# Pooling scores and pooling by 32-column operands into four row quarters of a bank, in an attention block fused with a rational feed-forward layer

## The chip, the cores and the metric

The kernel runs on one core of a Trainium2 chip. A core has five engines that work side by side, each with its own queue of instructions: TensorE (PE; its weight loads are listed apart as PEld), VectorE (DVE), ScalarE (ACT), GpSimd (POOL) and SyncE (SP), which issues all DMA transfers of this kernel in the order of its queue. The metric is the device time of one execution in microseconds (us), the median of several runs; lower is better.

## What is computed

Four batches (B=4) of N=12480 tokens with C=128 channels pass through an attention with m=32 inducing points, and then all 49920 tokens through a feed-forward layer of width 2048, whose activation is a quotient of two polynomials:

```python
def mab(q, kv):
    s = scale * (q @ kv.transpose(0, 2, 1))
    s = s - s.max(-1, keepdims=True)
    a = np.exp(s)
    a /= a.sum(-1, keepdims=True) + 1e-09
    return a @ kv
h = mab(I, x)            # pooling: 32 points attend to all tokens of a batch
x = mab(x, h)            # all tokens attend to the 32 pooled rows
...
h = x @ w_in
P = a[0] + a[1] * h + a[2] * h2 + a[3] * h3
Q = 1.0 + np.abs(b[0]) * np.abs(h) + np.abs(b[1]) * h2
g = P / (Q + 1e-06)
return (g @ w_out).astype(np.float32)
```

## The kernel before, in words

A batch is cut into 26 tiles of 480 tokens (BT; four chunks of TP=120), and tiles into groups of four (7 groups, the last with two tiles). The program has two stages.

**Boot** (`before`, lines 961 to 982, and the start of `main`): for batch 0 the pooling scores (`pass1`) and the pooling (`pooled`) are computed with nothing beside them, from wide tiles (xTw, xw); meanwhile the weights, 64-bit numbers in memory, are loaded (tiles `raw`) and converted on VectorE and POOL (`convert_weights`, with tiles cv). The loads are put between the steps of `pass1` and `pooled` by counts of those steps. `Params` loads moe_a and moe_b (tile `ab`) and VectorE derives the constants from them (tile `all`).

**Main** (`main`, `fast_ticks`): 832 units (4 batches, 26 tiles, 8 pairs of 128-wide slices of the 2048), one per tick. A unit's `first` makes hp with two f16 matmuls from the tile at (the attention weights of the tile's tokens, spread over 128 rows) and st (the pooled rows already multiplied by w_in); ACT, VectorE and POOL compute the activation (tiles u and l; ACT in turns Abs, Ln and Sigmoid); `second` adds two fp32 matmuls to po, the output bank. Once per tile VectorE copies po to oT and SP writes it to `out`.

Between the units of batch b stands side work, put there by `side` (line 780): two generators, `attend` (the tokens' attention: pd scores, pa transposes, hl, and eight copies of hl into at on SP's queue) and `ahead` (batch b+1: its pooling scores pc, the transposes pt, its pooling ph, then HT and the multiplication by w_in), announce before every step what it costs, as `yield "pe", 0.8`, in us of an engine, and `side` takes a step if the budget of that engine allows. PE's budget gains 0.75 per tick, keeps 2.5 at most, and 1.7 can be spent in a tick (line 193); so it is these costs that set the order. The side work's PSUM is one bank (`misc`), held by one generator at a time until `free`.

The two functions in question:

- `pass1` (line 370): the scores of four tiles come to stand below each other in one bank, pc, 32 rows each. Each tile's matmul writes all 128 rows, with a window of 128 columns out of `ind`, [128, 224], which is zero but for its 32 columns in the middle, and adds to what is there. VectorE takes the maximum (tile mxs) and copies to e.
- `pooled` (line 442): after the exponential (on ACT) four transposes (pt, copied to eT by ACT), then four matmuls per tile, one for each chunk, `eT` with 32 columns against the tile of 129 (128 channels and a column of ones that POOL's memset writes); all of a group add into ph[0:32], which VectorE adds to acc.

Tiles xTa (for pc) and x (for ph) are loaded in the order of use with four buffers, one tag: `columns` loads tile n+4 when tile n+1 is asked for, `x_rows` loads tile 4g+j+3 at tile 4g+j. So the load of a group's fourth tile is issued as the group's first matmul is. Before a group `landed` looks at the age of the fourth tile's load, in ticks, if it has been issued.

## Time and profile before

| | us |
|---|---|
| median of 3 runs | 2582.45 (2582.26 to 2583.76) |
| profiled execution | 2585.15 |
| its span, first to last instruction | 2583.0 |
| boot and the first units (to an Abs activation at 106.32) | 106.32 |
| units of batch 0, 1, 2 | 618.19, 624.43, 618.68 |
| units of batch 3 and the end | 615.38 |

| engine | busy us | share |
|---|---|---|
| PE | 2212.9 | 86% |
| DVE | 2219.0 | 86% |
| ACT | 2248.8 | 87% |
| POOL | 2070.8 | 80% |

The mean granted TensorE clock is 0.97 of full speed. The last stage has no work of a next batch in it; the three before it have. Nearly every instruction is recorded by one helper and shows as line 175, so tiles are the way to tell them apart. An engine's busy time does not tell what bounds the kernel; the windows below, cut at ACT's Abs activations (one for two units), tell what each engine does between them.

### The profile page before, as it was taken

The page shows a single profiled execution, that of the slowest core. Times are in us where ns is not written, and L with a number is a line of the kernel's source. Part 1 is how long each engine was busy: PE and PEld are TensorE (multiplying, and loading weights), DVE is VectorE, ACT ScalarE, POOL GpSimd, SP SyncE. Part 2 cuts the span into 40 slices and gives each one's busy share as a digit, 9 for nine tenths or more (in the row PEclk, how much of TensorE's full clock was granted, in tenths as well). Part 3 has the DMA queues.
Part 4 walks back from the last instruction along what each step waited for, and adds up shares of the span by engine and source line. Part 5 has one row for each costly group of instructions (what it writes and reads, how often), then busy time and mean ns, then how long its engine had stood idle before and what let it go on. Part 6 is the DMA issues. An engine that isn't in the chain of part 4 may idle for free.

```text
span 2583.0 us, 23703 instructions
## 1 busy us (share of the span) xinstructions
PE 2212.9 (86%) x7622; PEld 1074.2 (42%) x7622; DVE 2219.0 (86%) x2383; ACT 2248.8 (87%) x1591; POOL 2070.8 (80%) x1399
## 2 busy tenths in 40 slices
PE   8588987899889987998989989989878788788887
PEld 5344443454434443554534435544434334333333
DVE  2898998879889898889898989889989889888885
ACT  1388999988888899998898899998899999999995
POOL 0367789888868788888877887888788898899997
PEclk8689999999999999999998999999999999999999
DMA  9112210131112210221112202110101001000000
GB/s 249 54 58 80 71 37 16 38 77 43 31 45 75 76 39 13 56 62 43 42 58 69 65 23 54 51 49 27 49 13 46 20 15 31 15 17 18 12 15 17
DMA packets 117102, 120.88 MB, mean 47 GB/s; under 512 B 13289, under 2 KB 115561, under 8 KB 116969
## 3 DMA queue, kind: packets, MB, share of 16 engines
q1 hardware_dynamic: 116969, 119.28, 16.3%
q8 instruction: 62, 1.02, 0.2%
q14 instruction: 71, 0.58, 0.1%
HBM read 80.89 MB, written 25.56 MB: 41 GB/s over the span
## 4 chain that ended last, share of the span: by engine, by line
DVE 29%; PE 27%; POOL 21%; ACT 10%; issue 6%; DMA 1%; SPq 1%; DVEq 0%; POOLq 0%; ACTq 0%
DVE l L175 17%; PE po L175 16%; POOL l L175 15%; ACT u L175 8%; DVE u L175 6%; POOL u L175 5%; PE hp L175 4%; PE ph L175 2%; PE pd L175 2%; DVE oT L175 2%; ACT L175 2%; PE pc L175 1%; DVE asm L175 1%; SPq L175 1%; POOL a L175 1%
## 5 line engine op out<-in xcount | busy, mean ns | idle before, releaser
L175 PE MATMUL po<-l,w_out 128*128 128x480 f32 x3328 | 1485.6, 580 | 17.7 <-DVE oT L175 8.0
L175 POOL TENSOR_TENSOR l<-u 128x960 f32<-128x960 f32 x416 | 927.4, 2229 | 34.7
L175 PEld LDWEIGHTS po<-l,w_out 128*128 128x128 f32 x3328 | 627.3, 193 | 590.1 <-issue 457.2
L175 ACT ACTIVATE u<-u,all 128x1920 f32<-128x1920 f32 x416 | 775.5, 1888 | 1.2
L175 ACT ACTIVATE u<-u 128x1920 f32<-128x1920 f32 x416 | 737.5, 1797 | 8.2 <-POOL l L175 3.6
L175 POOL TENSOR_SCALAR l<-u,all 128x960 f32<-128x960 f32 x416 | 619.1, 1488 | 111.0 <-DVE u L175 105.1
L175 PE MATMUL hp<-at,st 128*128 128x480 f16 x1664 | 476.3, 374 | 266.7 <-DVE l L175 262.6
L175 DVE SCALAR_TENSOR_TENSOR l<-hp,all,l 128x960 f32<-128x960 f32 x416 | 504.1, 1212 | 185.3 <-POOL l L175 172.0
L175 POOL TENSOR_SCALAR u<-l,all 128x960 f32<-128x960 f32 x416 | 447.8, 1077 | 263.8 <-DVE l L175 229.3
L175 ACT ACTIVATE u<-hp,all 128x960 f32<-128x960 f32 x416 | 437.0, 1050 | 199.3 <-PE hp L175 180.6
L175 DVE SCALAR_TENSOR_TENSOR l<-l,all,u 128x960 f32<-128x960 f32 x416 | 575.0, 1383 | 1.7 <-ACT u L175 1.7
L175 DVE SCALAR_TENSOR_TENSOR l<-u,all,hp 128x960 f32<-128x960 f32 x416 | 500.1, 1202 | 6.2 <-ACT u L175 6.2
L175 DVE TENSOR_SCALAR u<-hp 128x960 int32<-128x960 int32 x416 | 475.7, 1144 | 17.6 <-PE hp L175 17.4
L175 PEld LDWEIGHTS <-st 128*128 128x128 f16 x1872 | 157.1, 100 | 711.4 <-DVE l L175 466.0
L175 ACT ACT_TABLE_LOAD x235 | 301.5, 1283 | 4.7 <-PEq L1056 0.7
L175 DVE COPY oT<-po 128x480 f32<-128x480 f32 x104 | 67.8, 652 | 81.5 <-PE po L175 81.3
L175 PEld LDWEIGHTS pd<-HT,xTb 128*120 128x120 f32 x832 | 102.5, 196 | 20.9 <-issue 9.1
L175 PE MATMUL pd<-HT,xTb 128*120 128x32 f32 x832 | 99.6, 275 | 7.0 <-DMA xTb<-x_c 6.1
L175 PE MATMUL ph<-x,eT 120*32 120x129 f32 x624 | 76.9, 274 | 3.5 <-DMA x<-x_t 3.5
L175 PE MATMUL pc<-xTa,ind 128*128 128x480 f32 x156 | 72.5, 570 | 5.6 <-DMA xTa<-x_c 2.8
L175 PEld LDWEIGHTS ph<-x,eT 120*32 120x32 f32 x624 | 64.9, 109 | 24.8 <-issue 16.3
L175 PE MATMUL po<-at,st 128*128 128x480 f16 x208 | 61.8, 380 | 0.0
(101 smaller groups left out, 685.9 us busy)
## 6 DMA issues: line engine op xcount, KB each, us to landing
xTb<-x_c SPq DMA_DIRECT2D x104, 240.0 KB, 2.9
out<-oT SPq DMA_DIRECT2D x104, 240.0 KB, 2.0
xTa<-x_c SPq DMA_DIRECT2D x78, 240.0 KB, 2.9
x<-x_t SPq DMA_DIRECT2D x78, 240.0 KB, 3.4
at<-hl SPq DMA_DIRECT2D x416, 30.0 KB, 1.8
xw<-x_t SPq DMA_DIRECT2D x8, 720.0 KB, 13.7
xTw<-x_c SPq DMA_DIRECT2D x5, 960.0 KB, 10.4
raw<-w_in SPq DMA_DIRECT2D x4, 480.0 KB, 11.7
```

Of the source, the lines that this page charges most:

```text
L175: ins = call(*args, **kw)
```

## The change

Three things. First, `ind` keeps only its 32 columns, and the four matmuls of a pc group write the four quarters of the bank's rows, each on its own (no accumulation, no zeros). They come after a single `yield "pe", 1.0` instead of four of 0.8, so that they stand in a row. Second, the four chunks of a tile in ph go to four quarters of the rows and accumulate over the tiles of the group; a tile announces 0.4 once where its four matmuls announced 0.2 each. acc has 128 rows, and at the end of a batch one matmul with `fold` (four identities of 32) adds the quarters: pq, from which the sum and H are read. Third, the counts by which boot puts the loads of weights between its steps are new, since there are fewer steps.

```diff
 
     def setup(self):
         nc, cp = self.nc, self.cp
-        self.ind = cp.tile([C, 7 * M], F32, name="ind")
-        nc.vector.memset(self.ind, 0.0)
-        nc.sync.dma_start(out=self.ind[:, 3 * M:4 * M], in_=self.ind_c)
+        self.ind = cp.tile([C, M], F32, name="ind")
+        nc.sync.dma_start(out=self.ind, in_=self.ind_c)
         self.ident = cp.tile([P, P], F32, name="ident")
         make_identity(self.tc.nc, self.ident)
         self.ones = cp.tile([1, 4], F32, name="ones")
...
         self.ident4 = cp.tile([M, 4, M], F32, name="ident4")
         for j in range(4):
             nc.vector.tensor_copy(out=self.ident4[:, j], in_=self.ident[0:M, 0:M])
+        self.fold = cp.tile([P, M], F32, name="fold")
+        for j in range(4):
+            rows = slice(M * j, M * j + M)
+            nc.vector.tensor_copy(out=self.fold[rows], in_=self.ident[rows, rows])
         self.many = cp.tile([M, 4], F32, name="many")
         nc.vector.memset(self.many, 1.0)
         self.w_max = cp.tile([C, 8], F32, name="w_max")
...
         for g in range(self.NG):
             nb = min(4, self.NB - 4 * g)
             yield from self.landed("a", b, g)
+            yield "pe", 1.0
+            pc = self.misc(f"pc{b}_{g}")
             for j in range(nb):
-                yield "pe", 0.8
-                if j == 0:
-                    pc = self.misc(f"pc{b}_{g}")
-                nc.tensor.matmul(pc[:, 0:BT], self.ind[:, M * (3 - j):M * (7 - j)], next(xs), start=(j == 0), stop=(j == nb - 1))
+                nc.tensor.matmul(pc[M * j:M * j + M, 0:BT], self.ind, next(xs), start=True, stop=True)
             rows = slice(0, M * nb)
             for i in range(2):
                 yield "v", 0.36
...
 
         nc, ap = self.nc, self.ap
         e = self.e[b]
-        acc = ap.tile([M, C + 1], F32, tag="acc", name=f"acc{b}")
+        acc = ap.tile([P, C + 1], F32, tag="acc", name=f"acc{b}")
         xs = self.xs.pop(b)
 
         def turned(g):
...
             yield from self.landed("x", b, g)
             for k in range(HB * nb):
                 j, c = divmod(k, HB)
-                yield "pe", 0.2
+                if c == 0:
+                    yield "pe", 0.4
                 if k == 0:
                     ph = self.misc(f"ph{b}_{g}")
                 if c == 0 and self.boot and (4 * g + j) % 3 == 0 and g + j:
...
                     self.wide_rows(b)
                 elif c == 0 and not self.boot and 0 < 4 * g + j < self.NB - 3:
                     xs.append(self.x_rows(b, 4 * g + j + 3))
-                nc.tensor.matmul(ph[0:M, 0:C + 1], eT[:, c, M * j:M * j + M], xs[4 * g + j][:, c, :], start=(k == 0), stop=(k == HB * nb - 1))
+                nc.tensor.matmul(ph[M * c:M * c + M, 0:C + 1], eT[:, c, M * j:M * j + M], xs[4 * g + j][:, c, :], start=(j == 0), stop=(j == nb - 1))
             yield "v", 0.2
             if g == 0:
-                nc.vector.tensor_copy(out=acc, in_=ph[0:M, 0:C + 1])
+                nc.vector.tensor_copy(out=acc, in_=ph[:, 0:C + 1])
             else:
-                nc.vector.tensor_tensor(out=acc, in0=ph[0:M, 0:C + 1], in1=acc, op=ALU.add)
+                nc.vector.tensor_tensor(out=acc, in0=ph[:, 0:C + 1], in1=acc, op=ALU.add)
             self.free()
-        yield "v", 0.2
+        yield "pe", 0.3
+        pq = self.misc(f"pq{b}")
+        nc.tensor.matmul(pq[0:M, 0:C + 1], self.fold, acc, start=True, stop=True)
+        yield "v", 0.4
         rs = ap.tile([M, 1], F32, tag="rs", name=f"rs{b}")
-        nc.vector.tensor_scalar(out=rs, in0=acc[:, C:], scalar1=1e-9, scalar2=None, op0=ALU.add)
+        nc.vector.tensor_scalar(out=rs, in0=pq[0:M, C:C + 1], scalar1=1e-9, scalar2=None, op0=ALU.add)
         nc.vector.reciprocal(out=rs, in_=rs)
         yield "v", 0.2
         H = ap.tile([M, C], F32, tag="H", name=f"H{b}")
-        nc.vector.tensor_scalar(out=H, in0=acc[:, 0:C], scalar1=rs, scalar2=None, op0=ALU.mult)
+        nc.vector.tensor_scalar(out=H, in0=pq[0:M, 0:C], scalar1=rs, scalar2=None, op0=ALU.mult)
+        self.free()
         yield "pe", 0.3
         pt = self.misc(f"HT{b}")
         nc.tensor.matmul(pt[:, 0:4 * M], H, self.ident4.rearrange("p a m -> p (a m)"), start=True, stop=True)
...
         self.setup()
         loads, words = self.weights(), []
         for n, _ in enumerate(self.pass1(0)):
-            if n >= 36 and n % 6 == 3:
+            if n >= 18 and n % 3 == 1:
                 words += [w for w in [next(loads, None)] if w]
         self.params = Params(self.tc.nc, self.cp, self.moe_a, self.moe_b)
         for n, _ in enumerate(self.pooled(0, self.cp.tile([C, 4 * M], F32, name="HT0"))):
-            if n % 20 == 5:
+            if n % 8 == 5:
                 words += [w for w in [next(loads, None)] if w]
         words += list(loads)
         self.params.derive()
```

What this does to the order. For batch 1 the scores' 7 groups begin 30 units into batch 0 and take 45 units before, 17 now; pooling's groups take 36 ticks before and 34 now; the multiplication by w_in starts 29, 47 and 68 units earlier for batches 1, 2 and 3. ACT's instructions are the same in number.

PE before, at the sixth group of batch 3's scores (pc3_5, tiles xTa3_20 to xTa3_23; hp2_4_7 is a unit of batch 2, tile 4):

```order
L175 MATMUL pc3_5_8260<-xTa3_20_8103,ind_74 128x480
L175 MATMUL pc3_5_8260<-xTa3_21_8118,ind_74 128x480
L175 LDWEIGHTS st_2_6700
L175 MATMUL hp2_4_7_8267<-at2_1_0_7888,st_2_6700 128x480
L175 LDWEIGHTS st_2_6700
L175 MATMUL hp2_4_7_8267<-at2_1_0_7888,st_2_6700 128x480
L175 MATMUL pc3_5_8260<-xTa3_22_8146,ind_74 128x480
L175 MATMUL pc3_5_8260<-xTa3_23_8261,ind_74 128x480
```

The group has a unit's hp between its second and third tile. PE after, at the same group, which now stands in batch 1's units, behind the last matmuls of po for tile 17:

```order
L175 MATMUL po1_17_0_6852<-at1_4_0_6144,st_1_3154 128x480
L175 LDWEIGHTS st_1_3154
L175 MATMUL po1_17_0_6852<-at1_4_0_6144,st_1_3154 128x480
L175 MATMUL pc3_5_6982<-xTa3_20_6934,ind_74 32x480
L175 MATMUL pc3_5_6982<-xTa3_21_6937,ind_74 32x480
L175 MATMUL pc3_5_6982<-xTa3_22_6940,ind_74 32x480
L175 MATMUL pc3_5_6982<-xTa3_23_6983,ind_74 32x480
L175 LDWEIGHTS st_1_3154
L175 MATMUL hp1_19_7_6993<-at1_4_1_6404,st_1_3154 128x480
```

All four now stand in a row, and the next unit's hp behind them. SP's queue at the loads of these tiles, before (out is a tile's result, at the eight copies of hl):

```order
L175 DMA xTa3_21_8118<-x_c 128x480
L175 DMA out<-oT2_1_8134 128x480
L175 DMA at2_1_1_8137<-hl2_1_7530 32x480 x8
L175 DMA xTa3_22_8146<-x_c 128x480
L175 DMA out<-oT2_2_8257 128x480
L175 DMA xTa3_23_8261<-x_c 128x480
L175 DMA xTa3_24_8264<-x_c 128x480
```

The copies stand ahead of the third tile's load, and one result between the third's and the fourth's. SP's queue at these loads, after:

```order
L175 DMA xTa3_20_6934<-x_c 128x480
L175 DMA xTa3_21_6937<-x_c 128x480
L175 DMA xTa3_22_6940<-x_c 128x480
L175 DMA out<-oT1_17_6970 128x480
L175 DMA at1_5_1_6973<-hl1_5_5949 32x480 x8
L175 DMA xTa3_23_6983<-x_c 128x480
L175 DMA xTa3_24_6986<-x_c 128x480
```

Now a result and the eight copies into at stand between the third tile's load and the fourth's, xTa3_23. At the sixth group of batch 3's pooling (ph3_5) it is the same, PE after:

```order
L175 MATMUL po2_3_0_8481<-at2_0_1_7718,st_2_6099 128x480
L175 LDWEIGHTS st_2_6099
L175 MATMUL po2_3_0_8481<-at2_0_1_7718,st_2_6099 128x480
L175 MATMUL ph3_5_8616<-x3_20_8516,eT3_5_8566 32x129 x4
L175 MATMUL ph3_5_8616<-x3_21_8523,eT3_5_8566 32x129 x4
L175 MATMUL ph3_5_8616<-x3_22_8530,eT3_5_8566 32x129 x4
L175 MATMUL ph3_5_8616<-x3_23_8617,eT3_5_8566 32x129 x4
```

All 16 matmuls stand in a row behind po's end; SP's queue after:

```order
L175 DMA x3_21_8523<-x_t 120x4x128
L175 DMA x3_22_8530<-x_t 120x4x128
L175 DMA out<-oT2_3_8604 128x480
L175 DMA at2_2_0_8607<-hl2_2_7756 32x480 x8
L175 DMA x3_23_8617<-x_t 120x4x128
```

where x3_23 stands behind out and the copies; before, these stood ahead of x3_21. At boot, SP's queue before (raw are weights, xw tiles of pooling, ab the activation's coefficients):

```order
L175 DMA raw0_177<-w_in 128x480
L175 DMA xw0_18_180<-x_t 120x12x128
L58 DMA ab_200<-moe_a 128x4
L59 DMA ab_200<-moe_b 128x2
L175 DMA raw1_216<-w_in 128x480
L175 DMA xw0_21_236<-x_t 120x12x128
L175 DMA raw2_244<-w_in 128x480
```

Between the first load of weights and the second stand ab and a tile of x; after:

```order
L175 DMA raw0_180<-w_in 128x480
L175 DMA xw0_18_184<-x_t 120x12x128
L175 DMA raw1_189<-w_in 128x480
L175 DMA raw2_199<-w_in 128x480
L58 DMA ab_208<-moe_a 128x4
L59 DMA ab_208<-moe_b 128x2
L175 DMA raw3_224<-w_in 128x480
L175 DMA xw0_21_244<-x_t 120x12x128
```

ab had one load of weights ahead of it and has three now.

## Rows read from the trace of the kernel before

**Rows 1.** The page: section 1 (each engine's busy time, share of the span, instructions) and the first line of section 4 (shares of the chain that ended last, by engine).

```profile
PE 2212.9 (86%) x7622; PEld 1074.2 (42%) x7622; DVE 2219.0 (86%) x2383; ACT 2248.8 (87%) x1591; POOL 2070.8 (80%) x1399
...
DVE 29%; PE 27%; POOL 21%; ACT 10%; issue 6%; DMA 1%; SPq 1%; DVEq 0%; POOLq 0%; ACTq 0%
```

**Rows 2.** Windows from one Abs activation of ACT to the fourth after it, nine of them near the end, with no work of the next batch in them. Columns: stretch, its length, busy time (and number) of PE, PEld, DVE, ACT, POOL, the granted clock, the DMA share, GB/s; the last line is sum and mean.

```profile
2415.95:2437.72 21.77, 17.65 (x50) 7.34 (x50) 19.02 (x18) 20.61 (x15) 20.26 (x13) 1.00 0.04 13
...
sum 195.77, PE 159.06 PEld 65.87 DVE 171.85 ACT 186.12 POOL 180.75; mean PE 17.67 PEld 7.32 DVE 19.09 ACT 20.68 POOL 20.08
```

**Rows 3.** The same view of the 18 such windows that hold matmuls of the pooling scores, the first from 173.38, the last to 1498.49; two of them and the sum.

```profile
872.98:899.38 26.40, 22.30 (x64) 10.18 (x63) 21.80 (x24) 21.16 (x17) 20.89 (x15) 0.94 0.20 61
...
1448.85:1475.05 26.20, 21.36 (x64) 9.54 (x65) 23.16 (x26) 21.17 (x16) 21.50 (x15) 1.00 0.21 65
...
sum 432.70, PE 392.13 PEld 184.16 DVE 394.56 ACT 384.38 POOL 348.78; mean PE 21.78 PEld 10.23 DVE 21.92 ACT 21.35 POOL 19.38
```

**Rows 4.** The same view of the 17 windows that hold matmuls of pooling, the first from 480.89; the last of them and the sum.

```profile
1684.59:1707.19 22.60, 22.29 (x96) 11.88 (x95) 18.77 (x19) 21.37 (x17) 20.29 (x16) 1.00 0.22 56
sum 392.63, PE 374.27 PEld 199.54 DVE 334.17 ACT 367.59 POOL 337.26; mean PE 22.02 PEld 11.74 DVE 19.66 ACT 21.62 POOL 19.84
```

**Rows 5.** Timeline of PE and its weight loads (PEld) at two pc matmuls. Columns: start, duration, engine, line, operation, out<-in, number of instructions run together.

```profile
895.49 1.77 PE L175 MATMUL pc<-xTa,ind 128*128 128x480 f32 x4
...
895.90 0.19 PEld L175 LDWEIGHTS pc<-xTa,ind 128*128 128x128 f32 x1 [0.21 <-issue]
896.30 0.19 PEld L175 LDWEIGHTS pc<-xTa,ind 128*128 128x128 f32 x1 [0.21 <-issue]
```

**Rows 6.** Timeline of the ph matmuls, at boot (32 instructions) and in the main stage (16, with a multiply by a wide operand before and after).

```profile
40.11 3.46 PEld L175 LDWEIGHTS ph<-xw,eT 120*32 120x32 f32 x32 [0.17 <-issue]
40.12 3.73 PE L175 MATMUL ph<-xw,eT 120*32 120x129 f32 x32
...
1688.45 1.96 PE L175 MATMUL ph<-x,eT 120*32 120x129 f32 x16
...
1690.34 0.58 PE L175 MATMUL hp<-at,st 128*128 128x480 f16 x2
```

**Rows 7.** The page, section 5, the ph matmuls of the main stage: operation, out<-in, count, busy time, mean ns of one, then idle time of PE before them and what ended it.

```profile
L175 PE MATMUL ph<-x,eT 120*32 120x129 f32 x624 | 76.9, 274 | 3.5 <-DMA x<-x_t 3.5
```

**Rows 8.** Timeline of VectorE: the maxima taken from the scores of four tiles (128 rows) and of two tiles (64 rows).

```profile
897.30 0.41 DVE L175 TENSOR_SCALAR_CACHE_REDUCE e<-pc 128x240 f32<-128x240 f32 x1 [0.58 <-PE pc L175]
...
909.53 0.39 DVE L175 TENSOR_SCALAR_CACHE_REDUCE e<-pc 64x240 f32<-64x240 f32 x1
```

**Rows 9.** Timeline at a pc group whose fourth tile came late: VectorE's copy of a result, SP's queue, PE, ACT. In brackets the idle time of the engine before it, and what ended it.

```profile
1464.16 0.65 DVE L175 COPY oT<-po 128x480 f32<-128x480 f32 x1
...
1464.84 0.35 SPq L175 DMA_DIRECT2D out<-oT  x1
...
1465.29 1.34 SPq L175 DMA_DIRECT2D xTa<-x_c  x3
...
1468.24 1.07 PE L175 MATMUL pc<-xTa,ind 128*128 128x480 f32 x2 [1.94 <-DMA xTa<-x_c]
...
1475.05 1.06 ACT L175 ACTIVATE u<-hp,all 128x960 f32<-128x960 f32 x1 [4.89 <-PE hp L175]
```

**Rows 10.** Timeline of SP's queue at the eight copies that spread `hl` into `at`.

```profile
1391.81 4.95 SPq L175 DMA_DIRECT2D at<-hl  x8
1396.86 0.53 SPq L175 DMA_DIRECT2D xTb<-x_c  x1
```

**Rows 11.** The page, section 6: DMA issues with their number, KB of one, and median us from issue to landing.

```profile
xTa<-x_c SPq DMA_DIRECT2D x78, 240.0 KB, 2.9
x<-x_t SPq DMA_DIRECT2D x78, 240.0 KB, 3.4
...
raw<-w_in SPq DMA_DIRECT2D x4, 480.0 KB, 11.7
```

**Rows 12.** Timeline of POOL's memsets of the ones column, with the ph matmuls between them.

```profile
1691.09 0.13 POOL L175 MEMSET x<- 120x4 f32 x2
...
1692.46 1.96 PE L175 MATMUL ph<-x,eT 120*32 120x129 f32 x16
...
1694.52 0.10 POOL L175 MEMSET x<- 120x4 f32 x1
```

**Rows 13.** Timeline of VectorE at boot: the first accumulation of pooling, the first instruction that reads `ab`, and the attention's first maximum.

```profile
39.64 0.28 DVE L175 COPY acc<-ph 32x129 f32<-32x129 f32 x1 [9.66 <-PE ph L175]
51.82 0.16 DVE L70 SCALAR_TENSOR_TENSOR all<-ab 128x1 f32<-128x1 f32 x1 [11.90 <-DMA ab<-moe_a]
...
93.72 0.69 DVE L175 TENSOR_REDUCE amx<-pd 120x16 f32<-120x512 f32 x1 [0.44 <-DVE w_out L175]
```

**Rows 14.** Windows at boot, columns as in rows 2.

```profile
28.00:32.00 4.00, 1.46 (x7) 1.22 (x8) 0.92 (x6) 1.99 (x3) 0.00 (x0) 0.86 1.13 183
...
64.00:68.00 4.00, 4.00 (x38) 3.96 (x38) 4.00 (x8) 0.38 (x1) 1.45 (x2) 1.00 1.09 351
```

**Rows 15.** Timeline of ACT and PE at an Abs activation that waited for hp.

```profile
898.71 0.97 PE L175 MATMUL hp<-at,st 128*128 128x480 f16 x4
...
899.38 1.06 ACT L175 ACTIVATE u<-hp,all 128x960 f32<-128x960 f32 x1 [2.57 <-PE hp L175]
```

## The prediction

> **What bounds the kernel now.** I read the page first: five engines are busy for 80 to 87% of the span, and the chain that ended last changes hands between VectorE (DVE), PE and GpSimd (POOL), ScalarE (ACT) being its fourth [rows 1]. So no engine's total decides; a stage must be read from who idles in it. Next I cut the span at the starts of ACT's Abs activations, which come once per two units, into windows of four such pairs, and sorted them by what side work lies in them. In nine windows near the end, with none of batch b+1's work, a window is 21.75 us and ACT is busy for 20.68 of it [rows 2]: ACT is the bound, with 1.07 us idle, and PE has 21.75 − 17.67 = 4.08 us to spare, 0.51 us in each of eight ticks. In the 18 windows with pooling scores (pc), ACT idles 432.70 − 384.38 = 48.3 us, where 18 calm windows would have 19.3: an **excess of 29.0 us** [rows 3]. In the 17 with pooling (ph) it idles 25.0 us against 18.2: an excess of 6.8 us [rows 4]. These 36 us are what faster side work can win at most. Not all of the 29 is PE's: in the pc windows VectorE is busy for 91%, with pooling's maxima and with the attention's own quotients, which the change leaves alone.
>
> **Scores (pc).** A pc matmul is two load-and-multiply pairs of 0.40 us each (a multiply from 895.49, the loads inside it at 895.90 and 896.30) [rows 5], so 0.80 us, and four tiles take 3.2 us whether they stand together or not. After, each writes one quarter of the bank's rows. No row shows two matmuls side by side in the array, so the bounds are: all four at once, 0.80 us; none, 3.2 us. I take the middle, because a matmul's two pairs use one quarter and must follow each other, while the second pair of one and the first of the next may overlap: five steps of 0.40, 2.0 us. Going from a wide operand to a 32-column one and back costs about 0.09 us each way: 16 pooling instructions take 1.96 us of PE in the main stage, where 32 took 3.73 without a change of width, 1.87 per 16 [rows 6]; so 2.19 us per group. The 6.5 groups of a batch then need 14.2 us. The built order puts them into 17 units of batch 1 where they took 45, and 17 ticks have 17 × 0.51 = 8.7 us of room. What is not covered is 5.5 us per batch, 16.5 in three; against 29.0 that is **−12.5 us** (all four at once: 6.4 us of work, all covered, and I keep 4 us for VectorE's share: −25; none: 22.2 us of work, 13.5 uncovered per batch: +11.5). VectorE's two maxima per group also come closer together; they are charged to its own budget as before, and the 4 us that I keep in the best case are for them. That HT is ready earlier in the order wins nothing here: I price it at 0.
>
> As for the array, the Trainium skill ("TensorE: Matmul & The Clock Gate", Part 3: Packing small matmuls — row/col tiling) lets tiles in different column quarters run side by side and gives a measured 2.38 times for three; no run here shows it yet, and by it a group would take 3.2 / 2.38 = 1.3 us, an estimate, and the sum would lie between the forecast and rival B. The same part, "What overlaps and what doesn't", speaks against this change: weight loads are said to lie beside a running multiply only if its rows differ, and all four operands here use the same rows. The trace disagrees: loads that use the same 128 rows as the multiply in progress start inside it [rows 5], so I give that rule no price of its own; if it held, the result would be rival D's.
>
> **Pooling (ph).** 16 matmuls are 32 instructions in 3.73 us [rows 6], 3.5 to 3.9 with the switch. In quarters the same overlap gives 17 × 0.11 + 0.19 = 2.06 us, a gain of 1.8 us of PE for each of some 20 groups. The excess is 6.8 us [rows 4], and PE's 3.5 us of waiting for x tiles [rows 7] are in it, so I take **−5 us** (0 to −7). VectorE's `acc` now adds 128 rows instead of 32; its time goes by the columns, as the maxima show: 0.41 us for 128 rows, 0.39 for 64 [rows 8], so 0. The new matmul `pq`, one per batch, has 129 columns as two of ph's instructions have, 0.23 us, and hands over through the bank that HT takes next; for three batches I count 0, at most 1 us.
>
> **Fourth tiles.** What it costs is that four matmuls now stand in a row, while the load of the fourth tile is issued as late as before, when the group begins. In the built order this falls behind the writing of a result and eight copies of `hl` at two places: `xTa3_23` and `x3_23`. Before, a late tile of this kind stopped PE for 1.94 us and ACT for 4.89 us at 1468–1475 [rows 9], so a stop of PE is not forgiven. The chain there: from the end of po, VectorE's copy until the queue issues, 0.68 us; the issue of `out`, 0.45 us with its gap [rows 9]; the eight copies, 4.95 and a gap of 0.1 [rows 10]; the landing, 2.9 us for xTa and 3.4 for x [rows 11]: 9.1 and 9.6 us. Three tiles' own matmuls cover 4 × 0.40 + 0.09 = 1.7 us of it, and 13 × 0.11 + 0.09 = 1.5. So PE stops for 7.4 and 8.1 us: **+15 us**. At five more places (`pc1_1`, `pc2_5`, `ph1_2`, `ph1_3`, `ph2_4`) the issue is one `out` and a landing away, 0.68 + 0.45 + 2.9 less 1.7, 2.3 us, or up to two ticks are between; I estimate 1 to 3.6 us each, 12 in all, and leave them to the range (+15 to +27; and down to +4, if hp is so far ahead that ACT has work). At `ph2_4` POOL's memset for `x2_19` also moves behind a unit's operations in its queue; memsets come 2.1 to 2.6 us after the ph before them starts [rows 6, 12], so it waits for POOL as much as for the load, and the 3.6 us covers both.
>
> **Boot.** The loads of weights come earlier by the new counts, and `ab` falls behind two more of 480 KB [rows 11]. VectorE has waited 11.90 us for `ab` at 51.82 and works from then on to 93.72, when the attention's maximum begins [rows 13], the conversions of the weights in between: what delays `ab` delays the end of boot. Two such loads are 983,040 bytes, at 183 to 351 GB/s [rows 14] 2.8 to 5.4 us; the engines of the DMA are full there (share 1.13 and 1.09), so an earlier issue does not bring the bytes sooner. Four accumulations, 0.28 us each as the first [rows 13], that stood behind `ab` now stand ahead of it, −1; acc5, acc6 and pq wait for PE between conversions, +1. **+4 us** (+2 to +6). The faster scores and pooling of boot bring nothing, as VectorE's work is behind `ab`. The constants (no memset of `ind`, four copies for `fold`) are early in VectorE's queue, ahead of a wait of 9.66 us [rows 13]: 0.
>
> **The sum.** 2582.45 + 4 − 12.5 − 5 + 15 = 2584 us. The profiled execution took 2585.15 us, 2.7 above the median, so differences are taken from it and put on the median. What can be told from no change is 0.2%, 5.2 us: this is 0.06%.
>
> **Rivals.**
> A, the forecast: pairs overlap, two fourth tiles stop PE. 2573 to 2595 by the bounds of boot (±2), of ph (+5, −2) and of the fourth tiles (−11, +4 of the smaller places). Chance 0.40, within it faster 0.08, same 0.26, slower 0.06.
> B, four quarters at once and fourth tiles mostly covered: pc −25, ph −7, tiles +4, boot +4: 2559 us. For it: the group is then 1 us, below two ticks' room. Against: the eight copies are in the queue whatever PE does. Chance 0.28, faster.
> C, **the late loads decide**: all seven fourth tiles stop PE in full, +27, pooling wins nothing since its tile is what it waits for: 2582.45 + 4 − 12.5 + 27 = 2601. It decides wherever the chain of the fourth load (4 us, or 9 with copies) is longer than the three matmuls ahead of it (1.5 to 1.8 us); below that it is nothing. For it: 1.94 us of waiting took 4.89 us from ACT [rows 9]. Against: ACT waited for hp for 2.57 us elsewhere with no tile late [rows 15], so a part of the 4.89 was due to other work. Chance 0.20, slower.
> D, the change does not do what it says: quarters of one bank run one after the other. A group is 3.4 us in one tick, charged as 1.0 by the planner. pc +11.5, ph 0, tiles 15 less 7 as each burst covers 1 us more, boot +4: 2606. For it: no row shows two matmuls at once. Chance 0.12, slower.
>
> **How the numbers follow.** The likeliest is A, so 2584 us. Faster 0.28 + 0.08 = 0.36; same 0.26; slower 0.06 + 0.20 + 0.12 = 0.38. The range goes from 2557, which leaves out about a third of B, to 2604, which leaves out D and little of C: 2 in 10 in all. A's own range is 2573 to 2595.
>
> **What will show it.** Pairs: the four pc multiplies of a group span 2.0 us; B: under 1.1; D: 3.2. In the pc windows ACT's excess falls to some 16 us. At the groups `pc3_5` and `ph3_5` PE idles 7 to 8 us until a DMA, at others 1 to 3. The wait of VectorE for `ab` ends near 55 us and the attention's maximum begins near 98. The forecast is wrong if the fourth tiles stop PE for under 4 us in all, or if boot ends no later than before, or if the pc group takes 3 us.

## The result and the profile after

| kernel | median us | ratio to before, 95% interval |
|---|---|---|
| before | 2582.36 (2579.63 to 2583.76, 4 runs) | |
| changed | 2606.69 (2603.27 to 2613.05, 4 runs) | 1.0098 (1.0075 to 1.0122) |

The change makes the kernel slower by 1.0%, 24 us. The profiled execution of the changed kernel took 2603.95 us, its span 2602.0; against the span before of 2583.0 that is 19.0 us to explain. The page after, busy time of the engines and the chain that ended last, answers to [rows 1]:

```profile
PE 2131.8 (82%) x7630; PEld 984.1 (38%) x7630; DVE 2228.4 (86%) x2386; ACT 2247.4 (86%) x1591; POOL 2053.1 (79%) x1399
...
DVE 33%; POOL 22%; PE 20%; ACT 13%; issue 7%; DMA 2%; SPq 2%; DVEq 0%; POOLq 0%; ACTq 0%
```

PE has 81 us less to do (2212.9 before), ACT as much as before and VectorE 9 us more, and yet the time is longer: PE idles 100 us more (370 before, 470 after). Where, the same cut by stage tells: boot, and the units of batches 0, 1 and 2 (batch 3 is unchanged at 615.4). Columns as in rows 2. Before:

```profile
0.00:106.32 106.32, 70.73 (x341) 48.61 (x341) 50.91 (x224) 13.91 (x24) 17.24 (x30) 0.79 0.73 179
106.32:724.51 618.19, 542.95 (x1977) 272.96 (x1977) 546.64 (x560) 555.23 (x396) 486.03 (x340) 0.97 0.17 50
724.51:1348.94 624.43, 551.56 (x1923) 269.71 (x1924) 553.52 (x576) 564.10 (x399) 513.74 (x354) 0.98 0.17 49
1348.94:1967.62 618.68, 549.11 (x1904) 267.69 (x1903) 547.69 (x552) 561.50 (x397) 508.24 (x350) 0.97 0.16 45
```

After:

```profile
0.00:113.40 113.40, 45.84 (x343) 24.09 (x343) 52.00 (x227) 13.90 (x23) 16.57 (x30) 0.62 0.69 168
113.40:750.97 637.57, 546.58 (x2037) 259.94 (x2038) 566.97 (x606) 556.21 (x397) 476.50 (x344) 0.94 0.20 58
750.97:1376.53 625.56, 530.09 (x1921) 246.51 (x1920) 549.82 (x561) 568.38 (x402) 501.61 (x354) 0.96 0.17 48
1376.53:1986.56 610.03, 510.71 (x1852) 238.17 (x1850) 538.55 (x522) 554.85 (x392) 512.97 (x345) 0.97 0.12 35
```

Boot is 7.1 us longer, batch 0 19.4, batch 1 1.1, and batch 2 8.7 us shorter. The column behind POOL's is the granted clock, and it fell: 0.97, 0.98, 0.97 before, 0.94, 0.96, 0.97 after, and at boot 0.79 before, 0.62 after. With 0.5 as the lower level (1.2 GHz of 2.4), a mean of 0.94 over 637.57 us is 12% of it, some 76 us, at half speed; 0.97 over 618.19 is some 37.

**The quarters do run at once.** Timeline of PE, a pc group of four tiles (eight instructions, with their weight loads) and a ph group (32):

```profile
194.30 0.16 PEld L175 LDWEIGHTS pc<-xTa,ind 128*32 128x32 f32 x8 [0.40 <-PE po L175]
194.30 1.01 PE L175 MATMUL pc<-xTa,ind 128*32 128x480 f32 x8
...
420.90 1.09 PE L175 MATMUL ph<-x,eT 120*32 120x129 f32 x32
```

1.01 us and 1.09 us, where before four tiles took 3.2 us (worked out in the prediction from [rows 5]) and 32 instructions 3.73 [rows 6]. That is rival B's price, not the forecast's 2.0 and 2.06.

**The waits.** The two groups of PE's instructions, with its idle time ahead of them in the last column and what ended it; first pc before, then pc and ph after:

```profile
L175 PE MATMUL pc<-xTa,ind 128*128 128x480 f32 x156 | 72.5, 570 | 5.6 <-DMA xTa<-x_c 2.8 <-DVE hl L175 1.8 <-issue 1.0
L175 PE MATMUL pc<-xTa,ind 128*32 128x480 f32 x156 | 31.5, 584 | 12.8 <-DMA xTa<-x_c 12.8
L175 PE MATMUL ph<-x,eT 120*32 120x129 f32 x624 | 25.3, 284 | 40.8 <-POOL x L175 26.8 <-DMA x<-x_t 13.6 <-ACT eT L175 0.4
```

Before, ph had 3.5 us [rows 7], with pc's 5.6 some 9 in all. After, it is 53.6 us, half of it for POOL, and nearly all of it is in the middle of bursts: in each of the 15 groups of pooling from a batch's second to its sixth PE stops ahead of the fourth tile, for 0.18 to 9.82 us, 13 times until POOL and twice until a DMA. One such stop, a group of pooling in batch 0 (SPq is SP's queue):

```profile
436.34 0.87 PE L175 MATMUL ph<-x,eT 120*32 120x129 f32 x24
436.88 2.39 SPq L175 DMA_DIRECT2D x<-x_t  x3
437.28 2.23 POOL L175 TENSOR_TENSOR l<-u 128x960 f32<-128x960 f32 x1
...
439.45 0.20 POOL L175 MEMSET x<- 120x4 f32 x4
...
439.60 0.66 PE L175 MATMUL ph<-x,eT 120*32 120x129 f32 x8 [2.40 <-POOL x L175]
...
440.19 3.10 PE L175 MATMUL po<-l,w_out 128*128 128x480 f32 x4
...
443.80 1.06 ACT L175 ACTIVATE u<-hp,all 128x960 f32<-128x960 f32 x1 [2.85 <-PE hp L175]
```

Three tiles' 24 instructions run at 436.34; the load of the fourth is issued at 436.88, and its memset stands in POOL's queue behind a 2.23 us operation of a unit. PE waits 2.40 us, released by POOL. And then the four instructions of po from 440.19 take 3.10 us instead of the 1.77 that four of po took at 434.63: PE had idled, and the clock that it is granted is down (0.66 on average from 440 to 444, below). ACT waits 2.85 us for hp behind it. Of the 15 stops eight were followed by such slow instructions, and the length of the stop alone does not tell which: behind another of 2.40 us, at 925.07, the four of po took 1.88. The other kind, the sixth group of batch 3's scores, of which the built order showed the loads:

```profile
1218.56 1.01 PE L175 MATMUL pc<-xTa,ind 128*32 128x480 f32 x6
...
1219.67 0.34 SPq L175 DMA_DIRECT2D out<-oT  x1
...
1220.07 4.95 SPq L175 DMA_DIRECT2D at<-hl  x8
...
1225.05 1.53 SPq L175 DMA_DIRECT2D xTa<-x_c  x3
...
1227.94 1.81 PE L175 MATMUL pc<-xTa,ind 128*32 128x480 f32 x2 [8.38 <-DMA xTa<-x_c]
...
1230.76 1.06 ACT L175 ACTIVATE u<-hp,all 128x960 f32<-128x960 f32 x1 [8.97 <-PE hp L175]
```

A result, eight copies in 4.95 us, and only then the load: PE stops for 8.38 us and ACT for 8.97. Windows of 4 us behind the first stop and over the second (the clock is the third column from the end):

```profile
440.00:444.00 4.00, 4.00 (x17) 1.81 (x10) 2.54 (x3) 1.15 (x2) 2.69 (x3) 0.66 0.27 69
1220.00:1224.00 4.00, 0.00 (x0) 0.00 (x0) 1.83 (x2) 1.80 (x1) 2.55 (x2) 1.00 0.32 100
1224.00:1228.00 4.00, 0.06 (x1) 0.06 (x2) 0.00 (x0) 0.00 (x0) 0.00 (x0) 0.54 0.51 148
1228.00:1232.00 4.00, 4.00 (x7) 1.31 (x8) 2.21 (x4) 1.24 (x2) 0.19 (x1) 0.60 0.36 121
```

At the second stop the clock falls to 0.54 while PE idles, and it is still 0.60 on average in the 4 us in which PE is wanted without a gap. In the windows with pc (ten now) and in those with ph (seventeen) the sums, answering to [rows 3] and [rows 4], are

```profile
sum 240.62, PE 216.60 PEld 90.65 DVE 216.14 ACT 210.77 POOL 180.86; mean PE 21.66 PEld 9.06 DVE 21.61 ACT 21.08 POOL 18.09
...
sum 411.79, PE 346.62 PEld 162.41 DVE 346.82 ACT 370.64 POOL 325.30; mean PE 20.39 PEld 9.55 DVE 20.40 ACT 21.80 POOL 19.14
```

pc: ACT idles 29.9 us, 10.7 of it natural, an excess of 19 instead of 29. ph: 41.2 us against 18.2, an excess of 23 instead of 6.8. What the scores won (10 us), pooling lost (16); boot comes on top. That is 13 of the 19.0 us; the other 6 are not traced to a place. VectorE at boot, the first use of `ab` and the attention's first maximum, against [rows 13]:

```profile
55.03 0.29 DVE L175 TENSOR_TENSOR acc<-ph,acc 128x129 f32<-128x129 f32 x1 [6.91 <-PE ph L175]
58.40 0.16 DVE L70 SCALAR_TENSOR_TENSOR all<-ab 128x1 f32<-128x1 f32 x1 [3.08 <-DMA ab<-moe_a]
...
100.74 0.69 DVE L175 TENSOR_REDUCE amx<-pd 120x16 f32<-120x512 f32 x1 [0.44 <-DVE w_out L175]
```

`ab` comes 6.6 us later than before, and the first maximum 7.0 us.

### The profile page after: what moved, and what is told of

Same layout as the page of the kernel before. It is cut to its first block, busy times and chain, and to the rows that moved or that the text cites. A ratio compares the mean times of both kernels' runs of the same rounds, so it can differ in the third digit from the quotient of the medians.

```text
span 2602.0 us, 23736 instructions
## 1 busy us (share of the span) xinstructions
PE 2131.8 (82%) x7630; PEld 984.1 (38%) x7630; DVE 2228.4 (86%) x2386; ACT 2247.4 (86%) x1591; POOL 2053.1 (79%) x1399
## 4 chain that ended last, share of the span: by engine, by line
DVE 33%; POOL 22%; PE 20%; ACT 13%; issue 7%; DMA 2%; SPq 2%; DVEq 0%; POOLq 0%; ACTq 0%
DVE l L175 19%; POOL l L175 16%; PE po L175 12%; ACT u L175 11%; DVE u L175 7%; POOL u L175 5%; PE hp L175 3%; ACT L175 2%; SPq L175 2%; DVE oT L175 2%; PE pd L175 2%; DVE asm L175 1%; DMA xTw<-x_c 1%; DVE cv L175 1%; DVE st L175 1%
## 5 line engine op out<-in xcount | busy, mean ns | idle before, releaser
L175 PEld LDWEIGHTS po<-l,w_out 128*128 128x128 f32 x3328 | 634.6, 195 | 603.2 <-issue 464.6
L175 POOL TENSOR_SCALAR l<-u,all 128x960 f32<-128x960 f32 x416 | 607.2, 1460 | 108.8 <-DVE u L175 107.5
L175 DVE SCALAR_TENSOR_TENSOR l<-l,all,u 128x960 f32<-128x960 f32 x416 | 585.2, 1407 | 1.7 <-ACT u L175 1.7
L175 PEld LDWEIGHTS pd<-HT,xTb 128*120 128x120 f32 x832 | 103.5, 198 | 20.1 <-issue 10.6
L175 PE MATMUL ph<-x,eT 120*32 120x129 f32 x624 | 25.3, 284 | 40.8 <-POOL x L175 26.8
L175 ACT ACTIVATE a<-a 120x512 f32<-120x512 f32 (+2 forms) x21 | 14.9, 728 | 41.2 <-DVE a L175 41.0
L175 POOL TENSOR_TENSOR cv<-cv 128x384 f32<-128x384 f32 (+2 forms) x11 | 12.1, 1096 | 48.5 <-DVE cv L175 47.0
```

Of the source, the lines that this page charges most:

```text
L175: ins = call(*args, **kw)
```

## The experiments

Theory: late fourth tiles (by the transfer and by POOL's memset) stop PE inside its bursts, and the clock that is granted after a stop adds to it; boot adds 7 us. Rivals: a PE with less to do gets less clock by itself; or side work pushed together costs, at VectorE. Each kernel is compared with the kernel before on the same chip, so ratios are compared. A tenth of a per cent is 2.6 us; by the intervals, a difference between two of these ratios is uncertain by 0.2 to 0.3%, 5 to 7 us.

| run | median us | ratio to before, 95% interval |
|---|---|---|
| e2_fourth_early | 2559.38 | 0.9903 (0.9887 to 0.9919) |
| e3_memset_late | 2576.87 | 0.9984 (0.9972 to 0.9997) |
| e9_fill | 2594.38 | 1.0061 (1.0045 to 1.0078) |
| e10_before_early | 2571.73 | 0.9968 (0.9958 to 0.9977) |
| e13_scores_early | 2566.41 | 0.9934 (0.9919 to 0.9948) |
| e4_scores_alone | 2587.53 | 1.0016 (1.0002 to 1.0030) |
| e5_pooling_alone | 2588.27 | 1.0010 (0.9997 to 1.0022) |
| e1_ab_back | 2606.02 | 1.0078 (1.0059 to 1.0097) |
| e7_both | 2551.43 | 0.9898 (0.9881 to 0.9915) |
| e8_before_ab_first | 2579.60 | 0.9980 (0.9968 to 0.9992) |
| e11_weights_early | 2566.37 | 0.9927 (0.9912 to 0.9942) |
| e12_weights_last | 2552.09 | 0.9876 (0.9857 to 0.9895) |

**e2_fourth_early.** In `columns`, `pass1` and `pooled`:

```diff
                 if n + 4 < self.NB:
                     ts.append(self.x_columns(b, n + 4, kind))
+                if kind == "a" and n % 4 == 3:
+                    yield None
...
                 nc.tensor.matmul(pc[M * j:M * j + M, 0:BT], self.ind, next(xs), start=True, stop=True)
+            if nb == 4 and not self.boot:
+                next(xs)
...
-                elif c == 0 and not self.boot and 0 < 4 * g + j < self.NB - 3:
+                elif c == 0 and not self.boot and j and 4 * g + j < self.NB - 3:
                     xs.append(self.x_rows(b, 4 * g + j + 3))
...
+            if not self.boot and 4 * g + 7 < self.NB:
+                xs.append(self.x_rows(b, 4 * g + 7))
             yield "v", 0.2
```

> The changed kernel, but the load of a group's fourth tile (and for pooling POOL's memset of its ones) is issued right behind the last matmul of the group before, not with the first matmul of its own. Theory (late fourth tiles cost the time): PE's idle time inside the bursts of the main stage, 12.8 us in pc and 38 in ph, falls below 5 us, and the time by 25 to 40 us, to 2567 to 2582; the granted clock's low stretches in the main stage, 162 us in the trace of the changed kernel against 108 before, go back with them to 100 to 120 us. Rival 1 (a PE that is less busy is granted less, whether it waits in bursts or not): the waits go but the low stretches stay near 160 us, and the time falls by 15 to 20 only, 2587 to 2592. Rival 2 (side work pushed together is what costs, VectorE above all): within 5 us of 2606.

Measured: 2559.38, 1.0% faster than before and 2% faster than the changed kernel; more than expected. Its groups of PE's instructions:

```profile
L175 PE MATMUL pc<-xTa,ind 128*32 128x480 f32 x156 | 22.1, 581 | 0.0
L175 PE MATMUL ph<-x,eT 120*32 120x129 f32 x624 | 21.9, 277 | 2.2 <-ACT eT L175 1.3 <-DMA x<-x_t 0.9
```

The waits are gone. By stage:

```profile
0.00:112.69 112.69, 47.28 (x343) 24.41 (x343) 51.77 (x227) 14.02 (x24) 17.20 (x30) 0.62 0.69 170
112.69:730.14 617.45, 526.06 (x1987) 253.71 (x1987) 558.29 (x576) 555.15 (x397) 481.14 (x341) 0.95 0.18 51
730.14:1336.16 606.02, 525.72 (x1966) 238.56 (x1966) 552.37 (x590) 562.05 (x396) 505.20 (x356) 0.99 0.21 59
1336.16:1941.32 605.16, 511.56 (x1854) 236.56 (x1854) 547.79 (x522) 560.07 (x395) 514.30 (x346) 0.98 0.13 36
```

Boot is as in the changed kernel; batches 0, 1 and 2 are 20.1, 19.5 and 4.9 us shorter than there, 44.5 in all, for 51.4 us fewer of waiting (53.6 less 2.2). The clock is back to 0.99 and 0.98 in batches 1 and 2; in batch 0 it stays at 0.95, which late tiles don't explain. Over the main stage the stretches at the lower level (low stretches, from here on) fall from 162 us in the changed kernel to 118, as the theory said; before they were 108. Rival 2 falls: the side work is pushed together as much. Rival 1 falls for batches 1 and 2, where PE has as little to do as in the changed kernel (525.7 and 511.6 us). The windows with pc (16) and ph (16):

```profile
sum 371.59, PE 323.53 PEld 137.06 DVE 348.42 ACT 342.07 POOL 300.49; mean PE 20.22 PEld 8.57 DVE 21.78 ACT 21.38 POOL 18.78
...
sum 353.95, PE 313.64 PEld 144.08 DVE 322.92 ACT 345.66 POOL 311.24; mean PE 19.60 PEld 9.00 DVE 20.18 ACT 21.60 POOL 19.45
```

pc: 29.5 us idle, 17.1 natural, an excess of 12; ph: 8.3 us, less than the 17.1 of as many calm windows.

**e3_memset_late.** As e2, but the memset of the fourth x tile stays with the first matmul of its group:

```diff
-        self.nc.gpsimd.memset(t[:, :, C:], 1.0)
+        if ones:
+            self.nc.gpsimd.memset(t[:, :, C:], 1.0)
...
+                elif c == 0 and not self.boot and j == 0 and 0 < 4 * g < self.NB - 3:
+                    nc.gpsimd.memset(xs[4 * g + 3][:, :, C:], 1.0)
...
-                xs.append(self.x_rows(b, 4 * g + 7))
+                xs.append(self.x_rows(b, 4 * g + 7, False))
```

> As e2_fourth_early, but POOL's memset of the fourth x tile's ones stays where the changed kernel has it, with the first matmul of its group; only the transfer is early. Theory (the memset is a part of the cost of its own, behind POOL's two operations of some 2 us each): PE idles for 20 to 35 us inside the ph bursts of the main stage, released by POOL, and the time is 8 to 20 us above e2_fourth_early, 2567 to 2580. Rival (the transfers are the whole cost; the memset's waits are covered by ACT's work in hand): within 4 us of e2_fourth_early's 2559.

Measured: 0.8% above e2 in the ratio, 21 us, and

```profile
L175 PE MATMUL ph<-x,eT 120*32 120x129 f32 x624 | 25.2, 285 | 29.9 <-POOL x L175 27.7 <-ACT eT L175 2.2
```

with 27.7 us of waiting for POOL. So the late memsets cost some 21 us where no transfer is late, and late transfers on top of them the rest up to the changed kernel, 1.0098 − 0.9984 = 1.1%, 29 us. The transfers late without the memsets were not run.

**e9_fill.** Work that adds zero (matmuls by `zero`, a tile of zeros) in the place of the waits, ahead of the fourth tile's matmuls:

```diff
+                if c == 0 and j == 3 and g and not self.boot:
+                    for i in range(32):
+                        rows = slice(M * (i % 4), M * (i % 4) + M)
+                        nc.tensor.matmul(ph[rows, 0:C + 1], self.zero, xs[4 * g + 2][:, i % 4, :], start=False, stop=False)
                 nc.tensor.matmul(ph[M * c:M * c + M, 0:C + 1], eT[:, c, M * j:M * j + M], xs[4 * g + j][:, c, :], start=(j == 0), stop=(j == nb - 1))
```

> The changed kernel with 32 matmuls by a tile of zeros ahead of the fourth tile's in every ph group but a batch's first and last: some 1.8 us of work for PE, which adds zero, in a place where it waits 1.4 to 9.8 us in 16 of 18 groups. Nothing waits for less. Theory (part of the cost is the clock that is granted less after PE has idled): low stretches in the main stage before batch 3 fall from 150 us to under 125, and the time by 4 to 15 us, to 2592 to 2602. Rival (the wait itself is all the cost): the time is 2604 to 2612, the fill adding a little where it outlasts the wait, with or without a change of the low stretches.

Measured: 0.4% faster than the changed kernel, 9 to 10 us, with 29 us of useless work added to PE:

```profile
L175 PE MATMUL ph<-x,zero 120*32 120x129 f32 x960 | 29.1, 273 | 0.0
L175 PE MATMUL ph<-x,eT 120*32 120x129 f32 x624 | 24.8, 280 | 20.6 <-DMA x<-x_t 14.0 <-POOL x L175 5.3 <-ACT eT L175 1.1
```

The same group as in the fence of the memset above:

```profile
432.81 0.87 PE L175 MATMUL ph<-x,eT 120*32 120x129 f32 x24
...
433.49 1.94 PE L175 MATMUL ph<-x,zero 120*32 120x129 f32 x64
...
435.94 0.22 POOL L175 MEMSET x<- 120x4 f32 x4
...
436.12 0.43 PE L175 MATMUL ph<-x,eT 120*32 120x129 f32 x8 [0.69 <-POOL x L175]
...
436.48 1.88 PE L175 MATMUL po<-l,w_out 128*128 128x480 f32 x4
```

The fourth tile's matmuls start 3.31 us after the group's first ones, 3.26 in the changed kernel: the wait is as long. Over all 15 groups that have the fill (not 18, as the expectation has it) these times add to 58.1 us, 4.7 more than in the changed kernel. But the four instructions of po behind this one take 1.88 us and not 3.10, and slow ones follow one of the 15 groups only, the one in which a stop of 8.29 us is left behind the fill. The low stretches of batches 0 to 2 fall from 150 us to 126 (under 125 was expected), and batch 0, where they fall most (75 to 55), is the one that becomes clearly shorter (637.6 to 628.7 us). So a part of the cost is the clock, at least about a fifth (9.5 of 50 us, with some 7 us of uncertainty): the fill leaves the scores' stops as they were (12.3 us) and takes time itself.

**e10_before_early and e13_scores_early.** The same early loads in the kernel before, and in the kernel before with the scores' part of the change (e4, below). In e10:

```diff
                 nc.tensor.matmul(pc[:, 0:BT], self.ind[:, M * (3 - j):M * (7 - j)], next(xs), start=(j == 0), stop=(j == nb - 1))
+            if nb == 4 and not self.boot:
+                next(xs)
...
-                elif c == 0 and not self.boot and 0 < 4 * g + j < self.NB - 3:
+                elif c == 0 and not self.boot and j and 4 * g + j < self.NB - 3:
...
+            if not self.boot and 4 * g + 7 < self.NB:
+                xs.append(self.x_rows(b, 4 * g + 7))
```

> The kernel before, with wide windows and its own order of steps, and only the loads of the fourth tiles issued early as in e2_fourth_early. Theory (quarters give a gain of their own, early loads the rest): PE's waits for x tiles, 9 us in pc and ph of before, go, and the time falls by 4 to 12 us, to 2570 to 2579. Rival (the gain of e2_fourth_early over before is all from early loads): 2555 to 2564.

> e4_scores_alone with the early loads of the fourth tiles of e2_fourth_early: the scores in quarters, pooling as before, nothing late. Theory (the scores' quarters carry most of the gain, as ACT's excess was 29 us in the windows of pc and 6.8 in those of ph): ratio to before 0.990 to 0.993, near e2_fourth_early's 0.9903 although pooling is as it was, boot being 6 us shorter here. Rival (both parts carry it alike): 0.994 to 0.997, near e10_before_early's 0.9968.

Measured: 0.9968 and 0.9934. The first is as the theory expected: late fourth tiles cost the kernel before 8 us too. Against e4 (1.0016), which has the same scores with late tiles, e13 is 0.8%, 21 us, faster for some 11 us of PE's waiting that is gone (11.5 in pc, 0.8 now in ph), and the low stretches of the main stage fall from 136 to 100 us: here the waits cost more than their length. The second is between what the two expected: the scores' quarters are worth 0.3%, 9 us, and the way from there to e2, pooling's quarters with the new counts of boot, 0.3% more, although boot is longer by them (112.7 us against 109.0). Each of the two is uncertain by some 5 us. So both parts carry the gain, and the rival is nearer.

**e4_scores_alone and e5_pooling_alone.** One part of the change each, with `ab` behind one load of weights as before. e4 is the kernel before with the diff's lines on `ind` and in `pass1`, and

```diff
-            if n >= 36 and n % 6 == 3:
+            if n == 19:
```

e5 is the kernel before with the diff's lines on `fold` and in `pooled`, and

```diff
-            if n % 20 == 5:
+            if n % 8 == 5:
```

> The kernel before with the scores' part alone (ind of 32 columns, four quarters, one step of 1.0); pooling as before, and ab with one load of weights ahead of it as before. Theory (quarters run at once; what costs is late tiles and ab): a pc group takes 1.0 us of PE instead of 3.2; the time is 2582 less 10 to 25, plus what the late fourth tiles of this order cost, 0 to 12: 2560 to 2582, not slower than before. Rival (side work pushed together costs): 2585 to 2600.

> The kernel before with pooling's part alone (chunks to four quarters, one step of 0.4 per tile, pq), the scores as before, ab with one load of weights ahead of it. Theory (POOL's memset and the load of the fourth tile come late in every group): PE idles for 25 to 40 us inside the ph bursts of the main stage, and the kernel is 10 to 25 us slower than before, 2592 to 2607. Rival (the loss is in the scores' part or in boot): within 5 us of 2582.

Measured: 1.0016 and 1.0010, both nearly the time before. The waits are where the theory put them (10.4 us for xTa in e4; 41.2 us in ph in e5, 23.0 of them for POOL), but the times miss it: e4 was expected 0 to 22 us faster than before and is 4 slower, a time that its rival also gives (the rival falls by e13, where the side work is the same and the time 21 us shorter); e5 was expected 10 to 25 us slower and is 3. In e4 the part's gain (9 us, e13 against e10) about pays for what the late tiles add; that it is so in e5 too is likely, but no run has pooling's part alone with nothing late. The two parts together with the old boot (e1) lose 0.8%, more than their sum of 0.3%; of these 13 us some lie in boot (111.9 us in e1, 104.8 and 108.4 in e4 and e5), the rest stays open.

**e1_ab_back.** One line of boot:

```diff
-            if n >= 18 and n % 3 == 1:
+            if n == 19:
```

> The changed kernel with one part undone: the counts of boot put the second and third load of weights behind ab again, so that ab has one such load ahead of it as in the kernel before. Theory (ab's place sets the end of boot): VectorE's first use of ab goes from 58.4 back to 51 to 53 us, the attention's first maximum from 100.7 to 93 to 95, and the kernel is 6 to 7 us faster than the changed one, 2600 us. Rival (the end of boot moved for another reason, as TensorE's low clock from 50 to 108 us): the first maximum stays within 2 us of 100.7 and the time within 2 us of 2606.

Measured: 0.2% below the changed kernel in the ratio, within the intervals of both. `ab` is used from 55.0 us, the first maximum is at 99.3: 1.5 us earlier, not 6 to 7. That is what the rival said (the maximum within 2 us of 100.7, the time within 2 of 2606). One execution shows it; the boots of the same program differ by up to 4 us between executions (e4 and e13 have one boot, 104.8 and 109.0 us). The cause that the rival names, the low clock at boot, is not shown: in e3, which has the changed kernel's boot, the clock there is 0.74 instead of 0.62 and boot is 3.8 us shorter, but its first accumulation comes 1.7 us earlier as well.

**e7_both, e8_before_ab_first, e11_weights_early, e12_weights_last.** `ab` loaded first of all, right behind `ind`, in e2 (e7) and in the kernel before (e8):

```diff
+        ab = self.cp.tile([P, 6], F32, name="ab")
+        self.nc.sync.dma_start(out=ab[:, 0:4], in_=self.moe_a.rearrange("(o n) -> o n", o=1).broadcast_to((P, 4)))
+        self.nc.sync.dma_start(out=ab[:, 4:6], in_=self.moe_b.rearrange("(o n) -> o n", o=1).broadcast_to((P, 2)))
         for n, _ in enumerate(self.pass1(0)):
```

e11 and e12 are e7 with other counts, first e11's, then e12's:

```diff
-            if n >= 18 and n % 3 == 1:
+            if n % 3 == 1:
```

```diff
-            if n >= 18 and n % 3 == 1:
+            if False:
...
-            if n % 8 == 5:
+            if n >= 58:
```

> e2_fourth_early, with the two small loads of ab issued first of all, right behind ind, and nothing else moved. Theory (VectorE's chain from ab sets the end of boot): VectorE derives the constants while pooling runs, the attention's first maximum comes 6 to 14 us earlier than at 98.4 us, and the time is 2545 to 2553. Rival (the landing of the weights sets the end of boot): the first maximum stays within 3 us and the time is 2556 to 2562.

> The kernel before with the two small loads of ab first of all, nothing else. Theory of the prediction (VectorE's chain from the landing of ab sets the end of boot): the first maximum comes 5 to 10 us earlier than at 93.7 us, and the time is 5 to 10 below before. Rival (e7_both gained 2 us of boot only: the weights' landing and their conversion set it): the first maximum within 3 us of 93.7, the time within 3 us of before.

> e7_both with the loads of weights spread over all of boot, one for every three steps of the scores from the first on, so that ten of the eleven stand ahead of the last two tiles of pooling. Theory (in boot the transfers are full, and what counts is whether VectorE's conversions can lie beside them): conversions run while pooling still loads, and the attention's first maximum comes at 80 to 90 us instead of 96.4; 2537 to 2547. Rival (pooling's own tiles set the end, since accumulations stand ahead of conversions in VectorE's queue): the first maximum at 96 to 104, 2551 to 2560.

> e7_both with all loads of weights behind all tiles of pooling. Theory: pooling ends some 8 us earlier, but the conversions, some 25 us of VectorE's time, begin when the first weights land, at 60 us or later, and the last weights land as late as before: first maximum at 96 to 104 us, 2551 to 2560. Rival (pooling's tiles set the end): at 85 to 92, 2540 to 2547.

Measured: the first maximum at 96.4 us in e7 (98.4 in e2), 93.6 in e8 (93.7 before), 107.5 in e11, 94.7 in e12. The theory that VectorE's chain from `ab` sets the end of boot falls, as far as one execution of each shows: with `ab` there from the start another wait takes its place. The time of e7 is e2's (0.9898 and 0.9903). That of e8 is 0.2%, 5 us, below before, as the theory said, though its first maximum is no earlier; where it comes from stays open (the execution in the trace, 2583.85 us, took 4 us longer than the median). In e11 the first maximum was expected at 80 to 90 us, or by its rival at 96 to 104: it came later than both. VectorE in e7:

```profile
65.52 0.29 DVE L172 TENSOR_TENSOR acc<-ph,acc 128x129 f32<-128x129 f32 x1 [6.63 <-PE ph L172]
...
96.41 0.69 DVE L172 TENSOR_REDUCE amx<-pd 120x16 f32<-120x512 f32 x1 [0.44 <-DVE w_out L172]
```

and in e12:

```profile
56.52 0.29 DVE L172 TENSOR_TENSOR acc<-ph,acc 128x129 f32<-128x129 f32 x1 [3.58 <-PE ph L172]
...
94.71 0.69 DVE L172 TENSOR_REDUCE amx<-pd 120x16 f32<-120x512 f32 x1 [0.44 <-DVE w_out L172]
```

An accumulation stands in VectorE's queue ahead of most conversions and waits for pooling's x tiles: 6.63 us until 65.5 in e7, where loads of weights are ahead of those tiles; in e12 the sixth is through at 56.5. The transfers are full in stretches of boot (shares of 1.13 and 1.09 before [rows 14]), so weights that come earlier hold up pooling (e11: ratio 0.9927 against 0.9898), and those that come last cost no more than those between (94.7 against 96.4). e12 has the best ratio of the study, 1.2% faster than before; its interval overlaps with e7's.

## Why the prediction was wrong

Forecast 2584, range 2557 to 2604; measured 2606.69. The mechanisms named were there, rival C's above all; what failed is the size of one term. The way from the kernel before over e10, e13 and e2 to the changed one gives the terms: −8 us for early loads, −9 for the scores, −8 for pooling with boot's loss, +50 for late loads and memsets, 25 in all.

- **Fourth tiles, +15: the step that failed.** The two places worked out (7.4 and 8.1 us) came as said, 8.38 at `pc3_5` and 9.82 at `ph3_5`. But the term stood for all late operands, and these cost some 50 us (e2), 42 more than in the kernel before (e10: 8 there). The step on `ph2_4` priced POOL's memset at one place. PE waits ahead of the fourth tile in all 15 groups, since `x_rows` issues the memset with the load, at the group's first matmul: 26.8 us of PE's waiting until POOL, 21 us of the time (e3). The row that says so was in hand: 2.1 to 2.6 us from ph's start to the memset [rows 6, 12], and ph in quarters is done with three tiles in 0.87.
- **The clock was not in the sum.** No term said that PE, having waited, can be granted half the clock when its work is there. At least 9 to 10 us (e9), part of the 50.
- **Scores, −12.5.** The step that lets a matmul's two pairs follow each other and neighbours overlap gave 2.19 us for a group; it takes 1.01 with all four at once. The rule of the Trainium skill on column quarters ("TensorE: Matmul & The Clock Gate", Part 3: Packing small matmuls — row/col tiling) agrees with the trace, 3.2 / 1.01 = 3.2 times for four tiles; the rule of "What overlaps and what doesn't", that weight loads need other rows to lie beside a multiply, does not: at 194.30 eight loads with the same 128 rows take 0.16 us together, at the head of the 1.01 us of multiplies. The gain nevertheless was about the term's, 9 us (e13 against e10), not the 25 of rival B: in e2 an excess of 12 us is left in the windows with pc, in which VectorE is busy for 94% (348.4 of 371.6 us). That VectorE is the cause is not shown.
- **Pooling, −5.** With operands in time 8 us, give or take some 5, together with boot's loss (e2 against e13), no less than the −7 that the excess seemed to allow: in e2 ACT idles less in ph windows than in calm ones.
- **Boot, +4.** +7.1 in the profiled execution; the same boot took 109.6 to 112.9 us in e2, e3 and e9, which is 3.3 to 6.6 more than before. The direction was right, the mechanism only in part: `ab` was the last wait, but the first maximum hardly moves with it (e1, e7, e8); in e7 pooling's tiles stand behind it, delayed by the loads of weights ahead of them (against e12). How the 7 us divide stays open.
- **The chances.** C was given 0.20, and its mechanism is the nearest, though it had seven late tiles and the trace has 18 (15 of pooling, 3 of the scores). What was weighed against it, that a part of ACT's 4.89 us was due to other work, did not help: a stop of PE of 8.38 us cost ACT 8.97, of 2.40 cost 2.85. That rival D's time, 2606, is the measured one to 1 us is luck: quarters that run one after the other are refuted by 1.01 us for a group. And A's lower bound is not the sum of its own bounds, which is 2569 and not 2573; nothing hangs on it.

## What to carry to other kernels

A group of operations that becomes three times shorter asks for its operands three times sooner: list every producer of each operand (transfer, memset, queue ahead of it) with the age it has at its use in the trace, and move the issues before the burst; here that step alone turned +1.0% into −1.0%. Look for the small instruction of another engine, issued together with a load: it waits in that engine's queue even when the load doesn't matter. And where transfers are full, order them by who waits in an in-order queue: a load moved forward is a load moved back.

## What was not expected of the hardware

Four fp32 matmuls of 32 columns, each two load-and-multiply pairs, run side by side in four row quarters of one PSUM bank: 1.01 us for what took 3.2. A stop of PE of 2.4 us was followed by half the granted clock, so that 1.77 us of multiplies took 3.10 (another of 2.4 us was not); with multiplies by zero in the stop they took 1.88, and a kernel with 29 us more of PE work was 0.4% faster.
